# Turning blocks 1 to 3 of x by VectorE and DRAM instead of TensorE, in an adaLN linear-attention and MLP block

## The chip, the cores and the metric

The kernel runs on one core of one Trainium2 chip. The metric is the device time of one execution in microseconds (us). The kernel before took 1138.91 us (median of 3 runs, 1138.76 to 1139.21).

## The reference

One block of a transformer on 2048 tokens of width 576. The parts that matter here:

```python
h = _layernorm(x, axis=-1) * (1 + ca) + sa          # sa, ca, ga, ... from silu(c) @ w_mod
qkv = h @ wqkv                                       # 576 -> 3 x 576, 32 heads of 18
pq, pk = phi(q), phi(k)                              # where(t > 0, t + 1, exp(t)) + 1e-6
kv = einsum("bhsd,bhse->bhde", pk, v); z = pk summed over the tokens
x = x + ga * ((pq @ kv) / (pq . z + 1e-6)) @ wo
h = _layernorm(x, axis=-1) * (1 + cb) + sb
x = x + gb * silu(h @ w1) @ w2                       # 576 -> 4608 -> 576
```

## The kernel before, in words

The 2048 tokens are 16 tiles of 128, in four blocks (0 to 3) of four tiles. A tile has its tokens on the 128 partitions. A product with a weight needs the width on the partitions instead, so a normalised block has to be turned: from four tiles of 128 tokens x 576 into five chunks (k = 0 to 4) of 128 features x 512 tokens. The tail of 64 features is written twice, which makes a tile 640 wide (DX) and the fifth chunk full. Every f32 operand is then split into a rounded part ("hi") and a remainder ("lo"), and a product is three passes: hi x hi, hi x lo, lo x hi. `modulate` (L195) applies scale and shift per feature on ScalarE, `split_h` (L203) writes hi by a cast on ScalarE and lo by a subtraction on VectorE (through `sub_hi`, L121), both into the block's hT.

The first part (up to about 205 us) goes over the tiles t = 0 to 15 (L642). For each tile it makes the k product (`k_proj`, L552, from t = 2), the v product (`v_proj`, L561), the sum over tokens of the tile before (`kv_mm`, L582), and a q product (`q_proj`, L577) while any of the first eight are left. k, v and q all run through `x_passes` (L222 to L226), which is why they share the line L226 in the profile: k has 28 matmuls of 352 and 288 columns in turn, v (from t = 2) 14 of 512, q 28 of 288. Their PSUM tiles are called psK, of which there are two.

Block 0 is turned while the weights come in (`turn_tiles`, `turn_half`, L387 to L401). Block tb + 1 is loaded at t = 4 tb (`load_x`, tiles xt, four rooms), normalised at t = 4 tb + 1, and turned chunk by chunk at t = 4 tb + 2 and + 3 by `turn` (L633): four TensorE transposes of 128x128 into one PSUM tile psT (`transpose_chunk`, L212, matmuls of line L214), then `modulate_split`. So blocks 1 to 3 take 3 x 5 sets of four transposes.

The modulation vectors come from w_mod: for block 0's two, columns are summed on VectorE and reduced by TensorE (L355 to L385); the later ones are loaded in 576 KB pieces called raw, with one VectorE step each into tmod (L508 to L521). The loaded f32 weights lie in acc[0..14] (`load_w`, L289) until they are split; later acc[t] holds q of tile t. wo is loaded into acc[11..15] (`load_wo`, L604).

The order of the work is not left to the code's order. `arrange` (L107) takes a table ORDERS of instruction numbers per engine and ties each instruction to the one before it in the table. For PE the table keeps the code's order but for ten matmuls in the start, and PE stands under a manual schedule besides. Each engine carries out its list strictly in order, and so does SP, which issues nearly all DMAs: an entry that waits holds up all behind it. A DMA also waits until an earlier one that used the same of eight completion semaphores (DMAHW0 to 7 below) has landed. The second part (attention output and the first MLP group, to about 370 us) and the main loop over the MLP (L1542 and after) follow; the main loop's order is fixed by its PLAN.

Of the kernel before, what the change touches and what calls it, by code (L numbers as in the profile page):

```python
# [22 lines left out]
def kernel(ctx: ExitStack, tc, A_x, A_wqkv, A_wo, B_x, B_w1, B_w2, c, w_mod, out):  # L23
# [28 lines left out]
    def f32(ap):  # L52
# [4 lines left out]
            0-106 114 107-109 115 110-113 116-2586  # L57
        """,
        "DVE": """
            0 3 2 1 4 6-7 11 8 12-13 9-10 14-16 18 17 5 19-22 30 23-24 28-29 25-27 43 31 44 33-34 36 35 37-38 32 39  # L60
            41 40 42 45-47 50 48-49 62-63 51-53 57 84 64 55 58 65 59 86 66 85 87 60 56 80 67 88 81 83 68 82 69 71 70
            72 122 73-74 61 89 54 75 78 76 90 77 79 123 91 124 92-93 96-97 125 98 94 126-127 100 99 95 101 103-104
            107 105 108 106 109 111 102 132-133 135 110 134 136 138-139 137 140-144 112 145 148 113 146 149 147 114
            117 115 118 116 119-121 128-129 131 150-151 225 223 130 226 224 222 152-155 157-158 156 159 162 176 160
            177-178 161 179-181 163 165 228 227 166-167 164 169-170 168 171-173 193-197 199 198 200 202 201 203-205
            174 209 206-207 210 208 175 182 185 183 186 188 187 184 189-190 192 191 211-213 216 214 217 215 218 220
            219 221 229 232 230 233 231 234-237 240 238-239 241-243 246 244 247 245 248-249 252 250-251 253-256 258
            257 259 263 260-262 266 268 267 270 269 271 264-265 272-273 275-277 274 281 279 282 278 280 283-284 288
            285 289 286 295-296 290 306 303 302 291 307 292 314 293 315 294 297 323 304 298-299 324 308 331 287 300
            309 301 310-311 305 312 316 332 340 313 317-319 341 320-321 325 351 322 326-329 352 362 330 333-336 338  # L70
            363 337 339 344 370 345-347 342-343 349 348 353 371 380 354-359 350 360 381 361 398 364-369 399 416
            372-375 377 376 378 417 424 385 382 384 379 387-388 391-392 394 425 402 386 389 403 390 404-407 393 383
# [1520 lines left out]
```

## Time and profile before

| | us |
|---|---|
| median of 3 runs | 1138.91 |
| span of the profiled execution | 1136.9 |
| TensorE (PE) busy in it | 1126.8 |
| VectorE (DVE) busy | 971.0 |
| ScalarE (ACT) busy | 538.7 |
| GpSimd (POOL) busy | 649.3 |

The span runs from the first to the last instruction of the profiled execution; the runs' time also holds what lies outside it. In a timeline's row stand the start, the length, the engine, the line, what is written from what, the shapes and the number of instructions merged into the row; in brackets how long the engine was idle before, and what released it. PEld is TensorE's loading of weights. "SPq" is SP issuing a DMA. In a window's row stand the busy time of each engine and its number of instructions, the granted TensorE clock, the share of the DMA engines' time and the GB/s. Matmuls are pipelined, so the length of one is its latency; how fast they follow each other is read from the starts.

### The profile page before, as it was taken

The numbers are of one execution on the slowest core, as the hardware profiler recorded it, in microseconds if no ns is written. First come the engines' busy times: TensorE is split into PE (matmuls) and PEld (weight loads), VectorE is DVE, ScalarE is ACT, GpSimd is POOL, SyncE is SP. The second block draws the span as 40 slices with busy tenths as digits, with TensorE's granted clock in tenths as the row PEclk, the third lists the DMA queues.
The fourth block names the chain that finished last, engine by engine and source line by source line (L and its number), as shares of the span: only waits on it lengthen the run. The fifth ranks groups of instructions, "written<-read, shape, count | busy, mean of one in ns | idle before, by whom it ended". The sixth has DMA issues, their size and how long they took to land.

```text
span 1136.9 us, 19287 instructions
## 1 busy us (share of the span) xinstructions
PE 1126.8 (99%) x7033; PEld 1040.8 (92%) x7033; DVE 971.0 (85%) x1543; ACT 538.7 (47%) x1112; POOL 649.3 (57%) x743
## 2 busy tenths in 40 slices
PE   8999999999999999999999999999999999999998
PEld 7999999999998899999999999999989999999998
DVE  6866744686878899999999999999999999999996
ACT  5643442547556544445445444444444444444441
POOL 1100000374714777767775776677667767776786
PEclk9999999999999999999999999999999999999999
DMA  9621100223359877976978869779778697697684
GB/s 281 199 84 31 44 7 1 71 84 116 137 198 354 340 274 256 348 278 257 361 261 315 314 250 356 273 255 364 261 277 331 265 344 281 258 346 274 256 310 156
DMA packets 58813, 269.03 MB, mean 237 GB/s; under 512 B 5724, under 2 KB 21856, under 8 KB 35680
## 3 DMA queue, kind: packets, MB, share of 16 engines
q1 hardware_dynamic: 58708, 267.80, 64.4%
q8 instruction: 56, 0.92, 0.3%
q14 instruction: 37, 0.30, 0.1%
q10 hardware_dynamic: 12, 0.00, 0.0%
HBM read 250.12 MB, written 16.78 MB: 235 GB/s over the span
## 4 chain that ended last, share of the span: by engine, by line
PE 94%; DMA 3%; DVE 1%; ACT 1%; POOL 0%; SPq 0%; issue 0%; POOLq 0%
PE up L1324 34%; PE down L1397 32%; PE psK L226 12%; PE big L226 7%; PE small L886 2%; PE big L897 2%; PE kvp L589 1%; DMA hT<-in_w_mod_dram 1%; PE big L812 1%; DMA raw<-in_w_mod_dram 1%; DMA hT<-hd 1%; PE small L214 1%; DMA xt<-in_A_x_dram 1%; PE up L1427 1%; PE down L1427 1%; PE psT L214 1%
## 5 line engine op out<-in xcount | busy, mean ns | idle before, releaser
L1405 DVE TENSOR_TENSOR acc<-down,acc 128x576 f32<-128x576 f32 x330 | 246.2, 754 | 13.2 <-PE down L1397 3.2
L1324 PE MATMUL up<-hT,w 128*128 128x512 f32 x916 | 239.4, 390 | 0.5 <-DMA hT<-hd 0.5
L1324 PEld LDWEIGHTS up<-hT,w 128*128 128x128 f32 x916 | 164.5, 188 | 25.4 <-DMA hT<-hd 0.7
L1359 POOL TENSOR_TENSOR s<-f,f 128x256 f32<-128x256 f32 x66 | 52.3, 792 | 159.7 <-ACT f L1340 159.7
L1397 PE MATMUL down<-w,hb 128*128 128x288 f32 x792 | 120.6, 294 | 0.0
L1397 PE MATMUL down<-w,hc 128*128 128x288 f32 x792 | 120.6, 294 | 0.0
L1397 PEld LDWEIGHTS down<-w,hc 128*128 128x128 f32 x792 | 113.7, 188 | 5.4 <-PE up L1324 0.3
L1397 PEld LDWEIGHTS down<-w,hb 128*128 128x128 f32 x792 | 113.7, 188 | 5.3
L121 DVE TENSOR_TENSOR w<-v,w 128x288 fp32r<-128x288 f32 (+1 forms) x170 | 114.8, 684 | 2.8 <-ACT w L1058 2.8
L1405 DVE TENSOR_TENSOR U<-down,U 128x576 f32<-128x576 f32 x132 | 99.6, 754 | 17.1 <-PE down L1397 15.2
L226 PE MATMUL psK<-w,hT 128*128 128x352 f32 (+3 forms) x506 | 106.4, 336 | 1.1 <-POOL w L317 0.6
L1324 PE MATMUL up<-room,w 128*128 128x512 f32 x348 | 91.0, 390 | 0.0
L1378 POOL TENSOR_TENSOR hc<-s,hc 128x512 fp32r<-128x512 f32 x66 | 89.4, 1355 | 0.1
L184 POOL TENSOR_TENSOR rstd<-ve,neghalf 128x4 f32<-128x4 f32 (+3 forms) x10 | 9.5, 953 | 138.8 <-DVE ve L183 138.8
L226 PEld LDWEIGHTS psK<-w,hT 128*128 128x128 f32 x506 | 81.8, 188 | 7.5 <-POOL w L317 0.8
L1340 ACT ACTIVATE f<-f 128x512 f32<-128x512 f32 x102 | 64.5, 632 | 47.8 <-DVE f L1345 24.8
L1343 DVE TENSOR_TENSOR f<-up,p 128x512 f32<-128x512 f32 x102 | 69.7, 683 | 12.1 <-PE up L1324 11.2
L1066 ACT CAST w<-v 128x288 fp32r<-128x288 f32 x85 | 36.7, 434 | 76.4 <-PE down L1397 62.1
L1324 PEld LDWEIGHTS up<-room,w 128*128 128x128 f32 x348 | 62.5, 188 | 9.4
L1363 POOL TENSOR_TENSOR f<-f,s 128x256 f32<-128x256 f32 x66 | 51.2, 776 | 34.9 <-DVE hb L1378 24.5
L1397 PE MATMUL down<-w,he 128*128 128x288 f32 x396 | 63.0, 294 | 0.0
L1397 PE MATMUL down<-w,ha 128*128 128x288 f32 x396 | 63.0, 294 | 0.0
(310 smaller groups left out, 2529.7 us busy)
## 6 DMA issues: line engine op xcount, KB each, us to landing
hT<-hd SPq DMA_DIRECT2D x66, 1280.0 KB, 5.5
hT<-hd SPq DMA_DIRECT2D x45, 1024.0 KB, 5.5
room<-hd SPq DMA_DIRECT2D x35, 1280.0 KB, 5.7
room<-hd SPq DMA_DIRECT2D x20, 1024.0 KB, 5.1
v<-in_B_w_dram SPq DMA_DIRECT2D x17, 576.0 KB, 7.2
v<-in_B_w_dram SPq DMA_DIRECT2D x17, 512.0 KB, 7.1
hd<-S SPq DMA_DIRECT2D x6, 1024.0 KB, 3.8
xt<-in_A_x_dram SPq DMA_DIRECT2D x16, 288.0 KB, 5.2
```

Source lines behind the costliest of these rows:

```text
L121: return V.tensor_sub(lo, full, f32(hi))
L214: T.transpose(ps[:, i * P : (i + 1) * P], xt[i][:, cidx * P : (cidx + 1) * P], ident)
L226: T.matmul(ps, xpart(a), wpart(b), start=n == 0, stop=n == len(XW) - 1)
L1066: A.copy(self.w2[n][:, 0], src)
L1324: T.matmul(ps, left, right, start=first and m == 0, stop=m == len(seq) - 1, skip_group_check=True)
L1340: A.activation(self.f[i, k], self.f[i, k], AF.Silu)
L1343: V.tensor_add(f, self.bank[bank[1]], self.p1)
L1359: G.tensor_add(self.s[:, 0:1], half(i, 0, 1), half(i, 1, 1))
L1363: G.tensor_sub(half(i, 1, 0), half(i, 1, 0), self.s[:, 1:2])
L1378: eng.tensor_sub(t[:, :, 1, :], src, f32(t[:, :, 0, :]))
L1397: T.matmul(ps[:, p, :HALF], self.a[i, n][:, u, p * P : (p + 1) * P], self.w.w2[n][:, v], start=n in (1, 5, 7, 6) and j == 0, stop=j == 2, ...
L1405: V.tensor_add(dst, ps[:, :, :HALF], dst)
```

## The change

For blocks 1 to 3 TensorE's transposes are gone. Each normalised tile (128 x 640) is written by one VectorE instruction into a scratch tile with every square of 32x32 turned in itself (`turn_tile`). Four DMAs, one per group of 32 partitions, store it into a DRAM tile xd such that the squares land in their turned places: each writes 32 x 20 runs of 32 numbers (128 bytes). One DMA loads xd back into a chunked tile `turned` (128 features x 5 chunks x 512 tokens). `turn` then only modulates and splits a chunk out of `turned`, in place; the tile h32 and PSUM's psT are no longer used there. `turned` and three scratch tiles lie in the second half of acc, which is one tile now. They share room with the raw q weights and with wo, so the split of the q weights stands before the first `turn_tile` in the code, and wo is loaded at t = 12 instead of 10. With three scratch tiles for four tiles of a block, the fourth uses the first one's.

All manual schedules of PE up to the main loop's first two units are lifted, and ORDERS is new for all engines; it now has a full order for PE. The numbers of matmuls but for the transposes, and those of the 28 dummy matmuls of the start (`warm_up`), are the same.

```diff
     ORDERS = {
         "PE": """
-            0-106 114 107-109 115 110-113 116-2586
+            37 0-2 38 3 8 4-7 9-15 19-20 29-36 21 16 22 39 25 40 26 17 72 18 73 41 78 23 43 45 24 79 42 44 27 47 46 28
...
-    accb = [accp.tile([P, 4, D], F32, name=f"acc{b}") for b in range(NB)]
-    acc = [accb[t // 4][:, t % 4, :] for t in range(NT)]
+    acca = accp.tile([P, NT, D], F32, name="acc")
+    accb = [acca[:, 4 * b : 4 * b + 4] for b in range(NB)]
+    acc = [acca[:, t, :] for t in range(NT)]
...
-    with tc.manual_schedule(engines={mybir.EngineType.PE}):
+    with nullcontext():
...
+    free = acca[:, QB : NT, :].rearrange("p t d -> p (t d)")
+    turned = free[:, : (KC + 1) * 512].rearrange("p (c t) -> p c t", t=512)
+    squares = [free[:, (KC + 1) * 512 + n * DX :][:, :DX] for n in range(3)]
+    xd = [dram.tile([KC + 1, P, P], F32, name=f"xd{n}") for n in range(4)]
+
+    def turn_tile(i):
+
+        y, d = squares[i % 3], xd[i]
+        V.transpose(y, xts[i])
+        for a in range(4):
+            rows = slice(32 * a, 32 * a + 32)
+            nc.sync.dma_start(d[:, :, rows].rearrange("c (b j) t -> j (c b) t", j=32), y[rows].rearrange("j (b t) -> j b t", t=32))
+        nc.sync.dma_start(turned[:, :, i * P : i * P + P], d.rearrange("c p t -> p c t"))
+
     def turn(tb, k):
-        ps = psT()
-        transpose_chunk(xts, k, ps)
-        h32 = pa.tile([P, 512], F32, name="h32")
-        modulate_split(ps, k, hT[tb], cols["a"], h32)
+        modulate_split(turned[:, k], k, hT[tb], cols["a"], turned[:, k])
...
+            if t == 1:
+                for k in START:
+                    split_w(wqp_, k, acc[10 + k], V)
...
                     ln.normalise(j, xts[j], xts[j], A if j % 2 else V)
+                    turn_tile(j)
...
             if t == 1:
                 turn_half((4,))
-                for k in START:
-                    split_w(wqp_, k, acc[10 + k], V)
...
-            if t == 10:
+            if t == 12:
                 load_wo()
```

On PE, around the last chunk's turning of block 1 and the first product of tile 4. In before, psT_811 is the fifth set of block 1, kvp the sum over tokens of tile 2, psK_830 is q3 and psK_871 the k product of tile 4, whose hT_490 is block 1:

```order
L226 MATMUL psK_792<-w_106,hT_102 128x512 x2
L214 MATMUL psT_811<-ident_85,xt_394 128x128
L214 MATMUL psT_811<-ident_85,xt_396 128x128
L214 MATMUL psT_811<-ident_85,xt_398 128x128
L214 MATMUL psT_811<-ident_85,xt_400 128x128
L589 MATMUL kvp0_108<-pk0_150,vx0_152 128x256
```

```order
L589 MATMUL kvp2_110<-pk0_150,vx0_152 128x128
L226 MATMUL psK_830<-wq_107,hT_102 128x288 x28
L226 MATMUL psK_871<-w_103,hT_490 128x352
L226 MATMUL psK_871<-w_103,hT_490 128x288
```

In the changed kernel psK_820 is q3, psK_861 the k product of tile 4, and hT_520 block 1:

```order
L306 MATMUL psK_820<-wq_104,hT_99 128x288 x10
L670 MATMUL kvp1_106<-pk0_147,vx0_149 128x256
L306 MATMUL psK_820<-wq_104,hT_99 128x288 x5
L306 MATMUL psK_861<-w_100,hT_520 128x352
L306 MATMUL psK_861<-w_100,hT_520 128x288
L306 MATMUL psK_861<-v_101,hT_520 128x352
L306 MATMUL psK_820<-wq_104,hT_99 128x288 x2
L306 MATMUL psK_861<-v_101,hT_520 128x288
L306 MATMUL psK_861<-w_100,hT_520 128x352
L306 MATMUL psK_820<-wq_104,hT_99 128x288
```

The set is gone, and the k product of tile 4 begins with nine matmuls of q3 still to come, which stand among its own.

On VectorE, the changed kernel's steps from block 1's second transpose to its fourth, with what each waits for (`a<-psK` at L413 evicts the k product of tile 2, vx_149 at L200 its v product, tmod is a step of the modulation):

```order
L722 STREAM_TRANSPOSE acc<-xt 128x640 [waits DVE_49]
L722 STREAM_TRANSPOSE acc<-xt 128x640 [waits Activation_49]
L258 BN_STATS st<-xt 128x6 [waits DMAHW1_49]
L413 TENSOR_SCALAR a<-psK 128x576 [waits PE_49,Activation_49]
L200 TENSOR_TENSOR vx_149<-psK,vx_149 128x64
L258 BN_STATS st<-xt 128x6
L722 STREAM_TRANSPOSE acc<-xt 128x640 [waits DMAHW4_49,DMAHW5_49,DMAHW3_49,DMAHW2_49]
L200 TENSOR_TENSOR vx_149<-psK,vx_149 128x4x126 [waits Activation_49]
```

The same evictions in before:

```order
L333 TENSOR_SCALAR a<-psK 128x576 [waits PE_49,Activation_49]
L121 TENSOR_TENSOR vx_152<-psK,vx_152 128x64
L121 TENSOR_TENSOR hT<-h_661,hT 128x512 [waits Activation_49]
L519 SCALAR_TENSOR_TENSOR tmod<-raw,sc,tmod 128x2x576 [waits DMAHW5_49,DVE_49]
L121 TENSOR_TENSOR vx_152<-psK,vx_152 128x4x126 [waits Activation_49]
```

Between the two evictions there now stands a transpose that waits for four DMAs, the stores of the block's first tile; the subtraction for block 1's first chunk (hT) has left this place for a later one.

On ScalarE, in the start: in before the load of the Exp table follows block 0's first casts and comes ahead of tmod's columns.

```order
L205 CAST hT<-raw 128x256
L431 ACT_TABLE_LOAD
L431 ACTIVATE warm<-sc 128x1
L368 COPY tmod<-tmod 128x64
L368 COPY hT<-hT 128x2x64
```

In the changed kernel it stands right ahead of the first exponential (e), behind three casts of weights; the casts of the last two v weights, which GpSimd's subtractions need, come after it:

```order
L389 CAST w<-acc 128x576 x3
L271 ACTIVATE xt<-xt,nm,rstd 128x64
L406 ACT_TABLE_LOAD
L406 ACTIVATE e<-psK 128x576
L389 CAST v<-acc 128x576
L271 ACTIVATE xt<-xt,nm,rstd 128x64
L390 CAST w<-acc 64x576
```

The dummy exponential (warm) that loaded the table early has moved to a place behind block 1's modulation.

Two moves more, in words: on SP the last modulation columns of block 0 (hT, 128x2x320, L287 before) are issued ahead of the second k weight tile, not behind it; and on PE the last transposes of block 0's tiles 2 and 3 (L390 before) stand behind 11 matmuls of q0 and four of the first kv product, not ahead of both.

More of the change, by code (lines that the diff above doesn't have):

```diff
@@ L1 @@
-from contextlib import ExitStack
+from contextlib import ExitStack, nullcontext
 from itertools import count
@@ L58 @@
+            2509-2510 2505 2514 2511 2515-2518 2520 2519 2521-2526
         """,
         "DVE": """
[L60 to L63, printed above, removed]
@@ L537 @@
     NP0 = 2
+    QB = NT // 2
     def xsel(t):
@@ L687 @@
                 tm = mod_piece(t // 3)
-            if t == 10:
+            if t == 12:
                 load_wo()
-    with tc.manual_schedule(engines={mybir.EngineType.PE}):
+    with nullcontext():
         qs = iter(range(QB, NT))
@@ L1219, in attn_step @@
                 lns[tb].normalise(i, xn2[tb][i], acc[4 * tb + i], A if tb < 2 or i in (0, 1) else V)
-    with tc.manual_schedule(engines={mybir.EngineType.PE}):
+    with nullcontext():
         for s in range(NT + 2):
@@ L1547 @@
     units = [(g, p) for g in range(1, NG) for p in range(2)]
-    with tc.manual_schedule(engines={mybir.EngineType.PE}):
+    with nullcontext():
         fetch(5)
```

153 lines of the change are left out of this document (117 added, 36 removed).

## The prediction

> **What bounds the kernel now.** I read the page first (shares of the engines, chain of waits), then the windows of 20 us, then TensorE's timeline over the stage that changes.
>
> ```profile
> span 1136.9 us, 19287 instructions
> PE 1126.8 (99%) x7033; PEld 1040.8 (92%) x7033; DVE 971.0 (85%) x1543; ACT 538.7 (47%) x1112; POOL 649.3 (57%) x743
> PE 94%; DMA 3%; DVE 1%; ACT 1%; POOL 0%; SPq 0%; issue 0%; POOLq 0%
> 0.00:20.00 20.00, 18.21 (x123) 17.03 (x124) 12.41 (x34) 9.03 (x17) 4.07 (x13) 1.00 0.91 276
> 20.00:40.00 20.00, 17.32 (x127) 16.25 (x126) 16.95 (x39) 18.19 (x40) 4.34 (x3) 1.00 0.68 204
> 40.00:60.00 20.00, 19.52 (x136) 18.65 (x135) 18.24 (x36) 8.47 (x17) 1.05 (x1) 1.00 0.80 235
> 100.00:120.00 20.00, 20.00 (x137) 19.05 (x136) 15.68 (x22) 11.56 (x21) 0.00 (x0) 1.00 0.16 45
> ```
>
> TensorE (PE) works in 99% of the span, and the chain that ended last is PE for 94%. Its idle time lies in the start: 1.8, 2.7 and 0.5 us in the first three windows, 5.0 of the span's 10.1. From 60 us on a window holds 20.00 us of PE work. There an instruction taken off PE shortens the span by its full pace, if what PE multiplies next is ready; nothing else gains anything. So two questions decide: what is a transpose worth on PE, and will the turned block be there when PE asks for it?
>
> **What PE gives up.** The 60 transposes (15 sets of four) and two tiles' periods, one without and one with sets:
>
> ```profile
> L214 PE MATMUL psT<-ident,xt x60: 270/272/289, 50.4 to 164.1; 128*128 128x128 f32 x60
> 69.81 3.94 PE L226 MATMUL psK<-wq,hT 128*128 128x288 f32 x28
> 82.03 3.93 PE L226 MATMUL psK<-wq,hT 128*128 128x288 f32 x28
> 109.49 3.93 PE L226 MATMUL psK<-wq,hT 128*128 128x288 f32 x28
> 113.26 0.60 PE L214 MATMUL psT<-ident,xt 128*128 128x128 f32 x4
> 117.80 0.60 PE L214 MATMUL psT<-ident,xt 128*128 128x128 f32 x4
> 121.45 0.60 PE L214 MATMUL psT<-ident,xt 128*128 128x128 f32 x4
> 122.99 3.94 PE L226 MATMUL psK<-wq,hT 128*128 128x288 f32 x28
> ```
>
> Between two q projections (28 matmuls of 288) stand one k, one v and one kv product. Without a set that takes 82.03 - 69.81 = 12.22 us. With the sets at 113.26, 117.80 and 121.45 it takes 122.99 - 109.49 = 13.50. So a set costs 1.28 / 3 = 0.43 us, 0.11 a transpose (the 272 ns are its latency, not its pace). Fifteen sets: **-6.4 us**. They lie in a stretch in which PE never idles, bar one: the set at 50.37 stands ahead of the wait at 51.45 below, which would swallow its 0.43 if VectorE freed the bank no earlier. The new order of VectorE has no long step of tmod ahead of that eviction, so I count the set in full and the wait of 0.48 as gone too: **-0.5** (bounds 0.4 and -0.5).
>
> **The start.** PE's waits between 20 and 52 us, ScalarE's table load, and a cast at the end of ScalarE's queue there:
>
> ```profile
> 22.18 0.80 PE L407 MATMUL psK<-w,hT 128*128 128x288 f32 x4 [1.25 <-ACT hT L205]
> 23.15 0.79 PE L407 MATMUL psK<-w,hT 128*128 128x288 f32 x4 [0.18 <-DVE hT L121]
> 28.24 0.44 PE L390 MATMUL psT<-ident,xt 128*128 128x128 f32 x2 [0.68 <-ACT xt L191]
> 32.48 0.81 PE L226 MATMUL psK<-w,hT 128*128 128x256 f32 x4 [0.57 <-POOL w L317]
> 51.45 0.50 PE L226 MATMUL psK<-w,hT 128*128 128x512 f32 x1 [0.48 <-DVE acc L333]
> 13.92 1.28 ACT L431 ACT_TABLE_LOAD   x1
> 28.09 0.66 ACT L309 CAST v<-acc 128x576 fp32r<-128x576 f32 x1
> 220.00:370.00 150.00, 148.81 (x1052) 142.19 (x1051) 119.59 (x210) 88.52 (x159) 76.79 (x73) 1.00 0.49 175
> ```
>
> The waits of the first four rows sum to 2.7 us. Two moves act on them. The late modulation columns are now loaded ahead of the second k weight tile: 295 KB fewer before them, at the first window's 276 GB/s 1.1 us earlier, which the wait of 1.25 (for hT, made with these columns) could give back. Against it, the load of the Exp table, 1.28 us at 13.92 in a stretch where ScalarE had time, now stands right before the first exponential, among casts that follow each other without a gap up to 28.09 and that feed GpSimd, for which PE waits at 32.48. So -1.1 and +1.3: I take **0**, with -2.7 (every wait gone) and +1.3 (the table load in full) as ends. The order of the later stages is new as well, but from 220 to 370 us PE idles only 150.00 - 148.81 = 1.2 us, so I give it nothing.
>
> **The turned block's way.** A block's five chunks were made by PE, a step of ScalarE and so on, chunk by chunk. Now each tile takes a VectorE transpose, four stores of 80 KB in 640 runs of 128 bytes, a load of 320 KB, and then the same three steps per chunk. Blocks 2 and 3 are turned a whole tile period (12 us) before use, so their cost is hidden. Block 1 has no such room. The rows for it:
>
> ```profile
> 38.67 7.66 PE L226 MATMUL psK<-wq,hT 128*128 128x288 f32 x56
> 73.60 0.45 PE L226 MATMUL psK<-w,hT 128*128 128x352 f32 x2
> 37.65 0.81 SPq L260 DMA_DIRECT2D xt<-in_A_x_dram  x2
> 46.59 1.06 DVE L193 TENSOR_SCALAR xt<-xt,mv,rstd 128x576 f32<-128x576 f32 x2
> L1405 DVE TENSOR_TENSOR acc<-down,acc 128x576 f32<-128x576 f32 x330 | 246.2, 754 | 13.2 <-PE down L1397 3.2
> 13.47 0.55 DVE L360 TENSOR_SCALAR hT<-hT,sc 128x640 f32<-128x640 f32 x1
> 199.16 0.51 SPq L631 DMA_DIRECT2D a<-raw  x1
> pk<-raw SPq DMA_DIRECT2D x4, 72.0 KB, 2.1
> hd<-S SPq DMA_DIRECT2D x6, 1024.0 KB, 3.8
> acc<-in_A_x_dram SPq DMA_DIRECT2D x16, 288.0 KB, 2.7
> xt<-in_A_x_dram SPq DMA_DIRECT2D x16, 288.0 KB, 5.2
> L199 ACT ACTIVATE h<-psT,col_a x15: 772/785/798, 51.1 to 164.5; 128x512 f32<-128x512 f32 x15
> 51.92 0.62 ACT L205 CAST hT<-h 128x512 fp32r<-128x512 f32 x1
> ```
>
> *When PE needs it.* q0 starts at 38.67 and the first product of tile 4 (the first of block 1) at 73.60; with five sets and the wait gone that is 73.60 - 2.15 - 0.48 = 71.0. Nine of q3's 28 matmuls (0.135 each) now stand behind its start, which brings it to 69.8; its last chunk is due some 5 us later, about 74.7.
>
> *When it comes.* Tiles 2 and 3 were loaded at 37.65, once block 0's last transposes had freed their room. Those now stand behind 11 matmuls of q0 and four of kv, 2 us later: load at 39.7. Normalised tiles were there 10.0 us after the load (46.59 + 1.06), so 49.7. A transpose of 128x640 I price at 0.75 us, as the 754 ns of a 128x576 addition (bounds: 0.55, the 128x640 of one input at 13.47, and 1.5, two passes of the 754); four with the evictions that stand between them are through at about 55.5. SP issues a DMA of 32 partitions in 0.51; 16 stores and four others fill its queue from 50 to 60. A store lands after between 2.1 us (72 KB from 32 rows) and 3.8 (1 MB to DRAM): I take 3, nearer to the row with its shape, so 63. The load back takes 2.7 to 5.2: 3.5, so 66.5. ScalarE then spends 0.78 + 0.62 on a chunk, 7.0 for five, with 1.5 of evictions between them: last chunk at 75, due at 74.7. VectorE cannot be much earlier either: it is busy for 18.24 of the 20 us from 40 to 60 already, and gets 3 more. So the new wait lies between 0 and 3, more if a step is slower than priced; I take **+1.5**.
>
> The rule in the Trainium skill, VectorE: DVE Perf Modes, section The three transpose paths, speaks against the change, with the section Rules for kernel authors: VectorE turns only squares of 32, and for a whole 128x128 it advises TensorE. It gives 311 ns for 128x128 on VectorE in bf16; by it, an estimate, the 60 would take 18.7 us instead of 9.0, block 1 would come 3 us later and the time would be 1136.5. No row here shows a VectorE transpose.
>
> **The sum.** Span 1136.9 - 6.4 - 0.5 + 0 + 1.5 = 1131.5. The runs' median, 1138.9, stands 2.0 above the profiled span (the time outside it), so **1133.5**.
>
> **The rivals.**
>
> *The start gains too (0.15).* Interleaved orders fill PE's 2.7 us of early waits, and block 1 waits no more than 1.5. For it: the bytes moved behind the columns. Against: the table load. 1133.5 - 2.7 = 1130.8, or 1129.3 without any new wait.
>
> *Block 1 is late and eats the gain (0.18).* A new wait in place of the old work: 3 to 8 us, because SP's queue is strictly in order. A load back waits for its tile's four stores to land, and behind it stand the next tile's stores; each of the steps above slips by half a microsecond or two. For it: six estimated steps with no slack at their end. Against: the new PE order holds back q3 and kv products as fill at that place. Time: 1133.5 + 3 to 7 = 1136.5 to 1140.5, mostly within 0.2% of before.
>
> *Slow small stores: slower than before (0.12).* One mechanism at one place: the transpose of block 1's fourth tile writes into the room of the first, so it waits for that tile's stores to land, and VectorE's evictions stand behind it.
>
> ```profile
> q1 hardware_dynamic: 58708, 267.80, 64.4%
> ```
>
> A mean packet here takes 0.644 x 16 x 1136.9 / 58708 = 0.20 us of an engine, at 4.6 KB. If one of 128 bytes cost as much, a store's 640 on 16 engines would land after 8.0 us instead of 3. The fourth transpose would slip from 55.5 to about 60, its own stores by 5 more: block 1 some 9.5 us later, 1133.5 + 9.5 = 1143.0. Each microsecond of landing above 3 counts about twice, so the gain of 5.4 is gone at 5.7 us, and 0.2% is lost at 6.9. Against it: rows of 1 to 2.3 KB carried 276 GB/s at a share of 0.91 in the first window, and the page's mean packet of 4.6 KB makes 4.6 / 0.20 x 16 = 368 GB/s at full share: no steep fall. And 72 KB landed in 2.1. The Trainium skill, DMA: Bandwidth & Descriptors, section Specifications, is on its side: below 512 bytes an engine reads, modifies and writes back. By that rule the stores would be this rival's; no row of before has a store so small.
>
> **How the numbers follow.** The forecast has 0.55 and covers 1131 to 1136. A difference of 0.2%, 2.3 us, is about what a measurement of this kernel can tell from none. Faster than 1136.6: the forecast and the start's case, 0.70. Within 0.2%: late block 1, 0.18. Slower than 1141.2: slow stores, 0.12. The range runs from 1129.5 (waits of the start gone, a new wait near 0) to 1140.5 (block 1 late by 7 more); the slow stores are left out.
>
> **What would show it.** Right: no psT transposes of blocks 1 to 3 on PE; a period with q, k, v and kv of 12.2 us also at 110 us; PE idle between 60 and 80 us of 1 to 2 us, released by ScalarE or VectorE writing hT; transposes of about 0.75 us; stores landing in 2 to 4 us; the start's window of 20 to 40 us as full as before. Wrong: a PE wait above 5 us there; VectorE idle behind a transpose that a store released; a start more than 2 us longer or shorter; new waits after 220 us.

## The result, and the profile after

The changed kernel takes 1164.64 us (median of 4 runs, 1163.76 to 1165.8) against 1139.06 for the kernel before on the same chip. The ratio is 1.0221, interval 1.0204 to 1.0237: slower by 2.2%, 25.6 us, where I had forecast 5.4 us faster. In the figures below one execution of no_dram_trip, of 2244 us, is left out of the ratio but not of the median. First the page of the changed kernel: the span, the engines, the packets of the DMAs and the chain.

```profile
span 1163.7 us, 19292 instructions
PE 1133.7 (97%) x6973; PEld 1041.7 (90%) x6973; DVE 991.7 (85%) x1555; ACT 538.8 (46%) x1112; POOL 651.2 (56%) x743
DMA packets 98174, 276.90 MB, mean 238 GB/s; under 512 B 37404, under 2 KB 61216, under 8 KB 75040
PE 81%; DVE 7%; DMA 6%; ACT 2%; SPq 2%; issue 1%; POOL 0%; DVEq 0%; ACTq 0%; POOLq 0%
```

TensorE (PE) has 60 instructions less, as planned, and yet is busy for 6.9 us more; its idle time went from 10.1 to 30.0 us. So of 26.8 us of span 19.9 are new idleness; the rest is busy time, 6.9 us more where 6.4 were to go, some 13 us by which the same matmuls took longer. The chain shows who makes PE wait: VectorE's share went from 1% to 7%, the DMAs' from 3% to 6%, and the issuing on SP, which had nothing, has 2%. The windows, in the columns of those shown of before, say where:

```profile
20.00:40.00 20.00, 16.34 (x99) 15.29 (x98) 16.22 (x31) 15.11 (x29) 4.50 (x3) 0.83 0.54 170
60.00:80.00 20.00, 15.94 (x96) 14.71 (x96) 12.96 (x26) 6.59 (x14) 0.73 (x1) 0.91 0.76 181
100.00:120.00 20.00, 17.48 (x99) 15.89 (x98) 11.05 (x27) 9.19 (x17) 1.01 (x1) 0.91 0.64 153
140.00:160.00 20.00, 16.49 (x96) 14.26 (x95) 8.96 (x17) 8.55 (x17) 1.17 (x1) 1.00 0.35 87
220.00:370.00 150.00, 144.32 (x1013) 136.54 (x1012) 113.79 (x194) 84.94 (x151) 74.38 (x71) 0.99 0.38 136
360.00:380.00 20.00, 16.35 (x102) 14.17 (x100) 18.40 (x23) 14.46 (x28) 15.13 (x14) 1.00 0.81 297
380.00:400.00 20.00, 19.72 (x101) 17.12 (x101) 17.20 (x27) 7.60 (x15) 3.67 (x5) 0.91 0.68 249
```

Three of these windows in before:

```profile
60.00:80.00 20.00, 20.00 (x132) 18.95 (x132) 13.66 (x33) 9.75 (x19) 1.01 (x1) 1.00 0.25 86
140.00:160.00 20.00, 20.00 (x127) 18.57 (x127) 8.21 (x15) 8.79 (x17) 1.17 (x1) 1.00 0.00 1
360.00:380.00 20.00, 20.00 (x111) 17.64 (x110) 19.03 (x31) 10.57 (x24) 12.19 (x16) 1.00 0.92 338
```

Two places, not one. In the first part, 4.1, 2.5 and 3.5 us are lost in three windows of 20 us that had been full; behind it, between 220 and 370 us, PE idles 5.7 us instead of 1.2, and in the window from 360 to 380, which overlaps that one, 3.7. The clock column holds most of the rest: 0.83 and 0.91 in some of the windows that have waits in them or just before them, where it was 1.00 in before.

PE's waits up to 215 us, summed by what released them:

```profile
PE psK L306 <- DVE vx L200: 5.8, 3, 2.1
PE psK L306 <- DVE a L413: 2.7, 1, 2.7
PE psK L306 <- DVE mv L259: 2.4, 1, 2.4
PE psK L306 <- DVE col_b L608: 1.4, 1, 1.4
PE psK L306 <- ACT hT L285: 0.2, 1, 0.2
```

I had expected one wait, for the turned block (hT). PE never waits for that by more than 0.2 us. The 2.7 us (a) lie in the start, at 28.03. Behind 60 us PE waits for VectorE: for evictions of v products (vx), for a step of the statistics right behind such an eviction (mv, at 107.25), and for a column of the modulation (col_b, at 147.71, which stood behind 3.29 us of VectorE's waiting for a load of w_o). All these came late because VectorE, or the ScalarE step ahead of it, stood behind something else. The timelines show behind what. VectorE, SP and ScalarE, blocks 1 and 2; in brackets the idle time ahead of the row:

```profile
52.17 0.84 DVE L722 STREAM_TRANSPOSE acc<-xt 128x640 f32<-128x640 f32 x1
58.13 0.84 DVE L722 STREAM_TRANSPOSE acc<-xt 128x640 f32<-128x640 f32 x1 [0.35 <-DMA xd<-acc]
...
85.30 0.84 DVE L722 STREAM_TRANSPOSE acc<-xt 128x640 f32<-128x640 f32 x1
97.56 0.84 DVE L722 STREAM_TRANSPOSE acc<-xt 128x640 f32<-128x640 f32 x1 [3.54 <-DMA xd<-acc]
105.30 0.82 DVE L258 BATCH_NORM_STATS2 st<-xt 128x6 f32<-128x288 f32 x2 [5.35 <-DMA xt<-in_A_x_dram]
...
53.42 3.75 SPq L725 DMA_DIRECT2D xd<-acc  x6
57.22 0.53 SPq L340 DMA_DIRECT2D xt<-in_A_x_dram  x1
60.55 3.77 SPq L725 DMA_DIRECT2D xd<-acc  x4
64.41 0.45 SPq L340 DMA_DIRECT2D xt<-in_A_x_dram  x1
68.29 2.90 SPq L726 DMA_DIRECT2D acc<-xd  x3
...
75.56 0.81 ACT L279 ACTIVATE acc<-acc,col_a 128x512 f32<-128x512 f32 x1 [7.55 <-DMA acc<-xd]
147.78 2.93 ACT L279 ACTIVATE acc<-acc,col_a 128x512 f32<-128x512 f32 x4 [5.82 <-DMA acc<-xd]
```

Block 1's first transpose starts at 52.17, its first chunk is modulated (L279) at 75.56: the trip takes 23.4 us. Block 2's takes 113.36 - 85.30 = 28.1, block 3's, from 117.12, 30.7. ScalarE stands 7.55 us ahead of block 1's first chunk and 5.82 ahead of block 3's, with its casts behind. The loads of the next block's x (L340) lie scattered among the stores on SP, so VectorE's statistics (L258) wait for x, 5.35 us in one place, and the fourth transpose of block 2 waits 3.54 for the stores of the first. The rows for the transfers, from the view of the tile and from that of the DMAs:

```profile
L725 SPq DMA_DIRECT2D xd<-acc x48: 303/508/3185, 53.4 to 139.5; - x48
L726 SPq DMA_DIRECT2D acc<-xd x12: 359/388/778, 58.4 to 144.0; - x12
  ACT acc L279: 14.0, 3
  DVE acc L722: 4.5, 3
xd<-acc SPq DMA_DIRECT2D x48, 80.0 KB, 3.2
acc<-xd SPq DMA_DIRECT2D x12, 320.0 KB, 4.1
```

The last two rows hold the medians from issue to landing, of those DMAs whose landing the trace has (5 of the 48 stores and 3 of the 12 loads back): 3.2 us for a store and 4.1 for a load back, where I had 3 and 3.5. The longest store took 3185 ns to issue, the median 508. In that time SP issues nothing else; why that one was so slow, no view says.

### The profile page after: what moved, and what is told of

Its sections match the earlier page's. It is cut to its first block, busy times and chain, and to the rows that moved or that the text cites. A ratio compares the mean times of both kernels' runs of the same rounds, so it can differ in the third digit from the quotient of the medians.

```text
span 1163.7 us, 19292 instructions
## 1 busy us (share of the span) xinstructions
PE 1133.7 (97%) x6973; PEld 1041.7 (90%) x6973; DVE 991.7 (85%) x1555; ACT 538.8 (46%) x1112; POOL 651.2 (56%) x743
## 4 chain that ended last, share of the span: by engine, by line
PE 81%; DVE 7%; DMA 6%; ACT 2%; SPq 2%; issue 1%; POOL 0%; DVEq 0%; ACTq 0%; POOLq 0%
PE up L1417 32%; PE down L1490 31%; PE psK L306 7%; PE big L306 5%; DMA xd<-acc 2%; SPq L725 1%; PE small L979 1%; DMA xt<-in_A_x_dram 1%; PE big L990 1%; DMA w<-hd 1%; DMA hT<-in_w_mod_dram 1%; PE kvp L670 1%; DMA acc<-xd 1%; ACT acc L279 1%; PE big L905 1%
## 5 line engine op out<-in xcount | busy, mean ns | idle before, releaser
L306 PE MATMUL psK<-w,hT 128*128 128x512 f32 (+3 forms) x506 | 117.5, 346 | 12.4 <-DVE vx L200 3.8
L200 DVE TENSOR_TENSOR w<-v,w 128x288 fp32r<-128x288 f32 (+1 forms) x170 | 117.1, 697 | 0.9 <-ACT w L1151 0.9
L306 PEld LDWEIGHTS psK<-w,hT 128*128 128x128 f32 x506 | 84.6, 194 | 20.3 <-issue 6.9
L1436 DVE TENSOR_TENSOR f<-up,p 128x512 f32<-128x512 f32 x102 | 69.6, 682 | 13.5 <-PE up L1417 11.6
L306 PE MATMUL big<-w,qT 128*128 128x288 f32 x352 | 71.4, 307 | 0.2
L1490 PE MATMUL down<-w,hd 128*128 128x288 f32 x396 | 63.9, 294 | 0.0
```

The costliest lines, as they stand in the source:

```text
L200: return V.tensor_sub(lo, full, f32(hi))
L306: T.matmul(ps, xpart(a), wpart(b), start=n == 0, stop=n == len(XW) - 1)
L1436: V.tensor_add(f, self.bank[bank[1]], self.p1)
L1490: T.matmul(ps[:, p, :HALF], self.a[i, n][:, u, p * P : (p + 1) * P], self.w.w2[n][:, v], start=n in (1, 5, 7, 6) and j == 0, stop=j == 2, ...
```

## The experiments

The theory after this look: two separate losses, one in the new order of the engines behind the first part, one in the trip through DRAM. The rivals: the late load of the Exp table as the source of everything that follows; one loss only, whose waits drag on; the 128-byte pieces.

**The order behind the first part, both ways.** second_part_old_order is the changed kernel with its order behind the first part put back; before_second_part_new is the kernel before with the new order there and nothing else. The tables' first lines that differ:

```diff
-  "PE": ... 1149 1155 1188 1167-1168 1184 1169 1189 1170 1192 ...
+  "PE": ... 1149 1155 1167-2526
```
```diff
-  "PE": ... 115 110-113 116-2586
+  "PE": ... 115 110-113 116-1226 1248 1227-1228 1244 1229 1249 ...
```

> The changed kernel with one thing undone: behind the first part (from the last half of q on, about 200 us) the instructions of every engine stand in the order of the kernel before; the first part, with the turning through DRAM, is untouched. Theory A (the new orders themselves cost time, wherever they stand): the start of the main loop lay 25.4 us late against 9.5 us at tile 15's k product, so about 15 us were lost in a stretch where nothing is turned; with the old order there 1148 to 1153 us. Theory B (the way through DRAM is late, and what comes behind only carries it on, as waits and a lower clock): 1161 to 1166 us.

> The kernel before, TensorE transposes and all, but with the instructions behind the first part in the order of the changed kernel. Theory A: the 15 us come here too, 1150 to 1156 us. Theory B: no more than 2 us from 1139, 1137 to 1141 us.

Measured: 1151.14 us (1149.83 to 1156.55), ratio 1.0128 (1.0101 to 1.0154); and 1150.55, ratio 1.0107 (1.0091 to 1.0123). So the new order costs 13.5 us taken out of the changed kernel, and 11.7 put into the kernel before, where no tile goes through DRAM. PE's longest waits of before_second_part_new from 220 to 425 us, and its windows:

```profile
PE small L842 <- DVE hT L77: 2.8, 2, 1.9
PE big L768 <- DVE v L273: 1.7, 1, 1.7
```
```profile
220.00:370.00 150.00, 141.84 (x982) 132.97 (x981) 120.39 (x196) 84.21 (x148) 78.02 (x73) 0.99 0.42 154
360.00:370.00 10.00, 8.09 (x36) 6.68 (x35) 9.85 (x11) 3.00 (x6) 5.93 (x4) 0.83 0.58 217
```

In the kernel before with its own order PE's waits there are four, of 0.2 to 0.4 us. Now 7.0 us go between 220 and 370 (150.00 - 141.84 = 8.2, against 1.2), spread over a few steps of VectorE that come late, and at 360 to 370 the clock stands at 0.83, which is 1.7 us more. The rest of the 11.7 is not accounted for.

**TensorE's order alone.** second_part_pe_old has the old order of PE behind the first part, and leaves the other engines' there as the change has them (the Exp table is loaded early in it).

> best_orders, computing all of it, with VectorE, ScalarE, GpSimd and SP behind the first part in the new order and TensorE alone in the old one. If the 12.5 us of the second part come from TensorE's new order (it asks for products before their inputs): 1148 to 1152 us. If they come from the orders of the engines that feed it, they stay: 1159 to 1164 us.

Measured: 1176.45 us, ratio 1.0314 (1.0284 to 1.0345). Both expectations missed. The new lists belong together: with PE's alone put back, PE waits for GpSimd's steps (3.9 us for pn) as well. Which engine's list makes the loss can't be read from exchanging this one.

**The trip.** no_dram_trip leaves out the 48 stores and 12 loads and lets the steps read VectorE's squares as they are, so that a block is turned only within its squares. Each of a block's four tiles has a room of its own in it, so no transpose waits for the stores of an earlier tile:

```diff
         y, d = squares[i % 3], xd[i]
-        V.transpose(y, xts[i])
-        for a in range(4): ...  nc.sync.dma_start(d[...], y[rows]...)
-        nc.sync.dma_start(turned[:, :, i * P : i * P + P], d...)
+        V.transpose(turned[tb % 2][:, i * DX : i * DX + DX], xts[i])
```

> The changed kernel with its 48 stores and 12 loads of the turning left out: VectorE still transposes squares, into a place of their own, and the split reads these (so the blocks of x are only turned within their squares of 32, and the output is not the reference's). All other orders stay. Theory B (the DRAM trip is what is late): the waits for blocks 1 to 3 and the SP queue's go, 8 to 15 us less, 1149 to 1157 us. Theory A: the first part's waits are mostly those of the orders, 0 to 4 us less, 1160 to 1165 us.

Measured: 1147.49 us, ratio 1.0078 (1.0061 to 1.0095). So without the trip the kernel takes some 17.1 us less.

**The Exp table.** exp_table_early puts the dummy exponential back to where it loads the table before block 0's columns are ready (ScalarE's table, `10-11` to `10 3 11`).

> The changed kernel with the small Exp of the start (it loads the table of Exp) put back to where ScalarE had it before the change, behind its second split of block 0, so that the table is there before tile 0's Exp. If the load of 1.28 us at 25.2 us stands on the path at the start (theory A's smallest part): 1162 to 1164 us, 1 to 2 us less. If it is covered: 1164 to 1165.5 us.

Measured: 1163.14 us (1162.14 to 1164.79) against 1164.64 (1163.76 to 1165.8); ratio 1.0219 (1.0203 to 1.0234) against 1.0221. The load then lies at 15.19 instead of 25.24. The medians differ by 1.5 us, but the runs overlap, and the ratios don't tell the two apart. In the profiled executions the early table puts the k product of tile 3 1.4 us ahead of the changed kernel's, and the end of the first part 0.2 us behind it. And second_part_old_order, with the late table, came to tile 3 no later (58.3 us) than best_orders below with the early one (58.9). So a price of its own for the table load is not shown, and it starts nothing bigger.

**Do the parts add up?** best_orders is the changed kernel with the second part's old order and the table early; no_trip_best_orders is the same without the transfers.

> The changed kernel, computing all of it, with both undoings that were tried alone: the old order behind the first part, and the small Exp early. If the parts add up: 1164.6 - 13.5 - 1.4 = 1149.7, 1148 to 1151.5 us. If the Exp's gain is covered by block 1's wait, as the lag of exp_table_early at tile 4 suggests: 1150 to 1152 us.

> best_orders with the way through DRAM left out as in no_dram_trip (output not the reference's): what the change would be worth if the transport cost nothing. If the parts add up: 1147.5 - 12.5 - 1.4 = 1133.6, 1132 to 1136 us, some 5 us under the kernel before, as 15 sets of four transposes at 0.43 us would have it. If something else in the new first part eats the gain: 1137 to 1139 us.

Measured: 1148.99 us, ratio 1.009 (1.006 to 1.012), and 1133.6, ratio 0.9958 (0.9942 to 0.9973). They do, within 1 us of what was expected; but for the order and the table load together that means 15.7 us, of which the 1.5 of the table is not shown. The longest of the last one's TensorE waits up to 215 us, and a window:

```profile
PE psK L183 <- DVE w L272: 1.6, 1, 1.6
```
```profile
60.00:80.00 20.00, 20.00 (x129) 18.57 (x129) 18.96 (x38) 10.98 (x22) 1.36 (x1) 1.00 0.21 72
```

A full window at clock 1.00, and so are those at 100 and 140 us, with VectorE's transposes in them. By TensorE's first step of the second part (for qT of tile 0, at 222.66 in before) this kernel is 6.47 us ahead: the 6.4 for the sets of transposes. That it fits to the tenth is partly luck, since up to there PE is busy 7.4 us less and idle 0.9 us more. Such starts make a table of where each kernel stands against before; here those of the k product of a tile, of qT, and of the main loop's 113th unit:

| us behind the kernel before | k, t = 4 | t = 5 | t = 8 | t = 10 | qT | main loop |
|---|---|---|---|---|---|---|
| changed kernel | 4.9 | 8.1 | 7.2 | 13.1 | 12.5 | 27.3 |
| best_orders | 3.1 | 6.3 | 5.3 | 10.7 | 9.8 | 10.0 |
| no_trip_best_orders | -4.6 | -1.8 | -7.2 | -5.6 | -6.5 | -6.4 |
| before_second_part_new | -0.6 | -0.6 | -0.6 | -0.9 | -0.7 | 11.8 |

The difference of the two middle rows is the trip's price: 8.1 us by t = 5 (block 1), 12.5 by t = 8 (block 2), 16.3 from t = 10 on (block 3). Each block pays, block 1 about half.

**Is it the wait for the data?** trip_aside issues all 60 transfers, with the loads back into a place that no step reads (four of the five chunks, 256 KB instead of 320); the steps read the squares. As in no_dram_trip, a block's tiles have four rooms, so the fourth transpose's wait for the stores (4.5 us of VectorE in the changed kernel) is gone as well.

```diff
-        nc.sync.dma_start(turned[:, :, i * P : i * P + P], d.rearrange("c p t -> p c t"))
+        nc.sync.dma_start(aside[tb % 2][:, i * 512 : i * 512 + 512]..., d[0:KC].rearrange("c p t -> p c t"))
-        modulate_split(turned[:, k], k, hT[tb], cols["a"], turned[:, k])
+        modulate_split(y, k, hT[tb], cols["a"], y)
```

> As no_dram_trip (the split reads the squares that VectorE wrote, so blocks of x are only turned within their squares and the output is not the reference's), but the stores and loads of the turning are issued as in the changed kernel, at their places in SP's order; the loads take four of the five column chunks and land where nobody reads them. What is left out is only the waiting for what they bring. Theory W (the split waits for a trip that takes long): within 3 us of no_dram_trip's 1147.5, 1146 to 1151 us. Theory Q (the 60 transfers hold up SP's queue, and with it the loads of x and of w_mod, or the memory): most of the 17 us stay, 1158 to 1165 us.

Measured: 1159.44 us, ratio 1.0178 (1.0142 to 1.0213). Of the 17.1 us only some 5 go with the wait for the data and the transpose's wait; some 12 stay with the transfers alone (the runs spread over 1156.18 to 1162.61). VectorE's wait for x in this kernel from 44 to 160 us, and SP's timeline:

```profile
DVE st L135 <- DMA xt<-in_A_x_dram: 9.7, 6, 5.3
```
```profile
53.80 3.66 SPq L602 DMA_DIRECT2D xd<-acc  x6
...
60.74 4.32 SPq L602 DMA_DIRECT2D xd<-acc  x4
65.16 0.45 SPq L217 DMA_DIRECT2D xt<-in_A_x_dram  x1
```

Without a reader of the turned block, 9.7 us still go to waits for x (8.5 in the changed kernel, none in no_dram_trip). SP issues from 53.4 to 72.5 almost without a gap, four stores alone in 4.32 us, and the loads of x (L217) stand where their turn comes.

**Another queue, and x ahead.** Both start from best_orders. turn_on_gpsimd_queue issues the 60 transfers from GpSimd (`nc.sync.dma_start` to `nc.gpsimd.dma_start`, orders to suit). x_loads_first moves the next block's x loads ahead of most stores on SP:

```diff
 DMA raw<-in_w_mod_dram 128x1152 x3
 DMA xt<-in_A_x_dram 128x576
-DMA xd_386<-acc 32x20x32 x4
-DMA xd_388<-acc 32x20x32
-DMA xd_387<-acc 32x20x32
-DMA xt<-in_A_x_dram 128x576
+DMA xd_386<-acc 32x20x32
+DMA xt<-in_A_x_dram 128x576
+DMA xd_386<-acc 32x20x32 x3
+DMA xd_388<-acc 32x20x32
+DMA xt<-in_A_x_dram 128x576 x2
```

> best_orders, computing all of it, with the 60 transfers of the turning issued on GpSimd's queue and not on SP's: the loads of x, w_mod and w_o stand on SP alone again, in the same order. GpSimd has three operations in this stretch, the power of each block's variance, and the transfers of a block stand behind that block's. Theory Q (what SP's queue holds up, the next block's x above all, on whose statistics VectorE waits in order, is most of the loss): of the 15.4 us between best_orders and no_trip_best_orders about 12 go, 1136 to 1141 us. Rival (the traffic itself, or the trip's own time, or GpSimd's slower issue): 1144 to 1151 us.

> best_orders, computing all of it, with nothing moved but the eight loads of x for blocks 2 and 3 on SP, 5 to 12 places forward, ahead of stores of the turning (at about 0.5 us of SP for a store, 2 to 6 us). Theory Q in its narrow form (x's loads, through VectorE's statistics): 3 to 8 us less than best_orders, 1141 to 1146 us. If it is the loads of w_mod or the traffic: 1147 to 1150 us.

Measured: 1152.55 us (1150.47 to 1153.61), ratio 1.0107 (1.008 to 1.0134), and 1157.47 (1155.25 to 1159.28), ratio 1.0148 (1.0116 to 1.0181), against best_orders' 1149.0. VectorE's waits for x are gone in both, and neither is faster: x_loads_first is some 8 us slower than best_orders, and both lie above every range that I had given. ScalarE's wait for the turned block, of best_orders and of x_loads_first:

```profile
ACT acc L156 <- DMA acc<-xd: 13.7, 3, 7.8
```
```profile
ACT acc L156 <- DMA acc<-xd: 20.3, 3, 7.8
```

What x gains, the turned block loses: 13.7 us of waiting became 20.3. On GpSimd's queue it is 16.9. The trip is long whichever queue carries it: from block 1's first transpose to its first chunk's modulation it takes 24.2 us on GpSimd's queue (48.37 to 72.55) and 23.7 on SP's in best_orders (50.15 to 73.83). GpSimd issues each store more slowly:

```profile
L602 POOL DMA_DIRECT2D xd<-acc x48: 682/682/1149, 49.5 to 138.8; - x48
```

**Longer pieces.** long_runs lets VectorE write its squares so that a row's five belong together: 640 bytes a piece in place of 128.

```diff
-        V.transpose(y, xts[i])
+        V.transpose(y.rearrange("p (b c t) -> p c b t", c=KC + 1, t=32), xts[i].rearrange("p (c b t) -> p c b t", c=KC + 1, t=32))
-            nc.sync.dma_start(d[:, :, rows]..., y[rows].rearrange("j (b t) -> j b t", t=32))
+            nc.sync.dma_start(d[a].rearrange("(b j) w -> j b w", j=32), y[rows].rearrange("j (b w) -> j b w", b=4))
```

> best_orders, computing all of it, with the turned squares laid out so that the transfers move pieces of 640 bytes instead of 128 (stores) and 512 (loads): VectorE writes a tile's squares grouped by their row of partitions, a store of 32 rows has 128 pieces and not 640, and the split reads 16 runs of 32 columns. The number of transfers, their bytes and their places stay, save 13 instructions around tile 9 that move by one to three places because a tile's run now holds all five chunks. If the many short pieces make the trip late: landings of the stores under 2.5 us and 3 to 7 us less than best_orders, 1143 to 1147 us. If the trip is late by its fixed time and SP's queue: within 1.5 us of best_orders.

Measured: 1150.17 us (1146.36 to 1151.43), ratio 1.0091 (1.0058 to 1.0123): no different from best_orders. The packets and the transfers' rows of long_runs:

```profile
DMA packets 72063, 276.91 MB, mean 241 GB/s; under 512 B 6684, under 2 KB 35104, under 8 KB 48928
```
```profile
L601 SPq DMA_DIRECT2D xd<-acc x48: 303/440/812, 50.8 to 131.3; - x48
DMA to landing us min/median/max: 1.8/3.6/6.0
```

Packets below 512 bytes fell to 6684, from the changed kernel's 37404. The last row takes stores and loads back together; the stores alone land after a median of 3.0 us, against 3.2 (5 of the 48 in each trace). The issue shrank, the longest from 3071 ns in best_orders to 812, the median from 506 to 440. At t = 8 this kernel was 4.7 us ahead of best_orders, and lost it again in block 3, where VectorE stood 5.2 us for w_o's loads. long_runs_late puts some of w_o's loads, and the steps that wait for them, behind block 3's transfers (SP's, VectorE's and ScalarE's tables):

> long_runs, computing all of it, with 19 places of VectorE's order, 13 of ScalarE's and 7 of SP's changed behind 135 us (from block 3's turning on): what stood behind the loads of w_o or behind block 3's loads back and needs nothing of them is taken ahead. long_runs was 4.7 us ahead of best_orders at tile 8 and lost it again at block 3, where w_o's loads must wait until block 3's last split is through, since a run of 640 bytes holds all five chunks. If that loss is the layout's own and goes with the order: 1149.0 - 4.7 = 1144.3, 1142 to 1147 us, and the short pieces are then 4 to 5 us of the 15.4. If the waits only move again, as in past_transfers: 1148 to 1151 us.

Measured: 1147.0 us (1145.2 to 1147.89), ratio 1.007 (1.0054 to 1.0087), the upper edge of what was expected. Longer pieces and this order together are worth some 2 us (and the interval overlaps with that of best_orders), not the trip.

**Orders that wait later.** past_transfers takes every VectorE and ScalarE step that waits for a transfer, or for a step on the trip, behind the steps that were ready; past_transfers_sp does it on SP too; long_runs_past joins the first's rule for VectorE and ScalarE with long_runs. VectorE's list of past_transfers against best_orders, around block 1's fourth transpose:

```diff
 STREAM_TRANSPOSE acc<-xt 128x640 x2
-BN_STATS st<-xt 128x6
 TENSOR_SCALAR a<-psK 128x576
 TENSOR_TENSOR vx_149<-psK,vx_149 128x64
-BN_STATS st<-xt 128x6
-STREAM_TRANSPOSE acc<-xt 128x640
+BN_STATS st<-xt 128x6 x2
 TENSOR_TENSOR vx_149<-psK,vx_149 128x4x126
 TENSOR_TENSOR vx_149<-psK,vx_149 128x8
+STREAM_TRANSPOSE acc<-xt 128x640
```

> best_orders, computing all of it, with TensorE, GpSimd and SP in the very same order and the same transfers. On VectorE and ScalarE, behind 44 us, instructions that stood behind one that waits for a transfer of x or of the turning (statistics, squares, splits) and need nothing of it were taken ahead of it, nothing else: 60 places of VectorE's order and 32 of ScalarE's differ. ready_first moved 177 and 121 places, the start among them, and lost. Theory L (the queue behind the first instruction that waits is part of the price): by the same arithmetic with landings 0.5 to 1 us longer than shown, 5 to 9 us less than best_orders at tile 15, and some clock: 1139 to 1144 us. Rival (the trip's length before block 1 and the traffic are all of it): 1147 to 1150 us.

> As past_transfers, and SP too may take up to three transfers ahead of one whose source is not there yet (16 of its places differ). By the arithmetic within 1 us of past_transfers; if SP's order is what holds the trip up, 2 to 4 us less than past_transfers: 1136 to 1141 us.

> long_runs, computing all of it, with the rule of past_transfers (VectorE and ScalarE alone, from 44 us on; SP as in long_runs). past_transfers was 3.4 to 6.0 us ahead of best_orders from tile 4 to tile 10 and gave all but 1.3 back by the end of the first part. If both gains hold: 1139 to 1143 us, about the kernel before. If the waits move: 1145 to 1150 us.

Measured: 1149.18 us (ratio 1.0082, 1.0055 to 1.0109), 1151.61 (1.0095, 1.0064 to 1.0126) and 1145.9 (1.0067, 1.005 to 1.0085). PE's waits up to 215 us, of best_orders, and then of past_transfers:

```profile
PE psK L183 <- DVE vx L77: 7.3, 3, 2.9
PE psK L183 <- DVE mv L136: 2.4, 1, 2.4
```
```profile
PE psK L183 <- ACT hT L162: 4.5, 1, 4.5
PE psK L183 <- DVE vx L77: 3.9, 2, 2.9
PE psK L183 <- DVE acc L290: 3.2, 2, 2.9
```

The waits at the heads of the queues are mostly gone (ScalarE's 13.7 us for the loads back are 0.5, VectorE's 9.8 us for x are 2.2), and in their place PE waits for the block itself, 4.5 us for hT: now the wait that I had looked for, since the evictions no longer stand behind it. The time is the same.

A fourth rule, ready_first, drew up VectorE's, ScalarE's and SP's lists anew by when each step could start, with ready_first_no_trip as its partner without transfers:

> best_orders, computing all of it, with the same instructions and transfers, TensorE in the same order; on VectorE, ScalarE and SP the first part was drawn up again by hand-written rule: going through the order of best_orders with the durations and landings that its trace shows (stores 3.3 us, loads back 3.9, x 3.2, issues 0.4 to 0.53), an engine takes the first of its next ten (ScalarE eight, SP two) instructions whose inputs are there, so that no engine stands behind a transfer while it has other work. Theory L (the trip is too long for the lead that the orders give it, and what costs is the queue behind the first instruction that waits, on VectorE for x's loads, on ScalarE for the loads back): the three waits of block 1 to 3 go, most of the 15.4 us between best_orders and no_trip_best_orders goes, 1134 to 1141 us. Rival (the traffic, or the trip's own length, which no order hides): 1145 to 1150 us.

> no_trip_best_orders (no stores and loads of the turning, output not the reference's) drawn up again by the same rule. It shows what the rule gains where there is no trip to hide: by its own arithmetic up to 6 us, half of them in the start; TensorE waited 3.4 us in all in the first part of no_trip_best_orders, so not more than about 4: 1129.5 to 1133.6 us. If ready_first falls by much more than this one, the order's gain there is the trip's.

Measured: 1166.4 us (ratio 1.0238, 1.0218 to 1.0257) and 1149.76 (1.0095, 1.0073 to 1.0117). Both lie above every range that I had given. The rule itself costs 16 us with no transfer in the program, 8 of them by tile 2 (53.2 us against 45.1 in no_trip_best_orders), so it tells nothing of whether an order can hide the trip; the pair's difference is 16.6 us once more. The best complete kernel with the turning by VectorE remains long_runs_past, 7.1 us behind the kernel before. No version found here beats it.

## Why the prediction was wrong

The parts, each from a pair of runs: -4.5 us for what TensorE no longer does (no_trip_best_orders, 1133.6 against 1138.1 for the kernel before on that chip), +15.4 for the trip (best_orders over it), +13.5 for the order behind the first part. That makes 24.4; measured, 25.6. What is left, 1.2 us, lies within the spread of the runs, and so does the 1.5 of the Exp table.

- *"-6.4"* for the fifteen sets was right as a sum: 6.47 at the end of the first part, with the luck told above. Of it the main loop loses some again: the profiled spans differ by 5.1.
- *"-0.5"* for the wait at 51.45 failed: the same wait of PE is still there, and longer, since the eviction that ends it (at 52.94) now stands right behind VectorE's first transpose (52.17).

```profile
53.71 0.50 PE L306 MATMUL psK<-w,hT 128*128 128x512 f32 x1 [0.73 <-DVE acc L413]
```

- *"From 220 to 370 us PE idles only ... 1.2 us, so I give it nothing"* failed, by 13.5 us. That idle time was a property of the old lists. It tells how little there is to gain from a new order, and nothing of what a new order can lose. I took a bound on the gain for a bound on both sides, and gave a part of the change that moves instructions on every engine neither a term nor a rival.
- *"Blocks 2 and 3 are turned a whole tile period (12 us) before use, so their cost is hidden"* failed, by 8.2 us of the 16.3. From the last transpose's end to the first split it takes 16.6, 15.0 and 12.5 us for the three blocks, more than the period on which I relied. More than that, I asked only whether the block would be there when PE wants it. What PE felt were the other queues: the statistics behind x, x behind stores, evictions behind a transpose that waits.
- *"+1.5"* (0 to 3) for block 1 failed, by 6.6 us. Some sizes were nearly right: 0.84 us a transpose (0.75), landing 3.2 and 4.1 (3 and 3.5). The block's first chunk was modulated at 75.56, where I had the load back there at 66.5. The transposes were through at 58.97 (55.5), and SP's queue was mis-sized: I had it full from 50 to 60, with 20 DMAs, and it issued from 53.0 to 71.8, 26 DMAs with x loads, w_mod's and loads back among the stores, so the last loads back went out from 68.29 on (63). And I left out the steps behind a waiting one: ScalarE standing 7.55 us at the first split, with the casts for the evictions behind it.
- *The start, 0,* can't be told from right. TensorE came to tile 2 2.6 us later than in before and to tile 3 0.4 us later, and the 1.5 us between the medians with the table late and early are not clear of the spread (I had 1.3 as the upper end).
- *The rival "slow small stores"* had the sign, and a place that shows (VectorE stuck behind the fourth transpose, 4.5 us in three blocks). But in block 1, for which it had its price, that wait was 0.35 us, so that its 9.5 stands near the measured 8.1 is luck. Its cause was wrong: the stores landed after 3.2 us and not 8, and pieces five times as long changed little. The Trainium skill, DMA: Bandwidth & Descriptors, section Specifications, says that below 512 bytes an engine reads, modifies and writes back; here stores of 128-byte pieces landed after 3.2 us and of 640-byte pieces after 3.0, so the landing shows next to nothing of it. What the longer pieces took away is time of issue.
- *The rule for whole 128x128 blocks* (the Trainium skill, VectorE: DVE Perf Modes, sections The three transpose paths and Rules for kernel authors) gave the right advice by another price. By its figure for bf16 the 60 blocks were, as an estimate, 18.7 us of VectorE; here twelve transposes of 0.84 make 10.1, and with the transfers left out (so with the squares not in their turned places) the kernel is 4.5 us faster than before. In the first part, what makes the change slower is the way through DRAM.

Three of the four signs announced as wrong came: VectorE idle behind a transpose that a store released, new waits after 220 us, and a start 2.6 us longer by tile 2 (0.4 by tile 3). The fourth, a PE wait above 5 us between 60 and 80, did not: there were two of 2.0 and 2.1.

What stays open: whether some order hides the trip. Six new orders moved its waits from queue to queue; the best of them won 3 us, together with the longer pieces. An earlier load of x, with more room for tiles, was not tried. How much of the 15.4 us is the queues and how much the traffic itself is open too. And it is not settled which list makes the second part's loss, only that it lies in those lists and not in the turning.

## What to carry to other kernels

When a change brings a new operation and a new order, price and test them apart: put the new order into the old kernel, and the old order into the new one. A full engine's small idle time bounds what an order can win, never what it can lose. And a detour by DMA isn't priced by its landing alone: count its issues on the queue and every step that stands behind a waiting one, on each engine, since the wait shows up under another name than the tile that is late.

## What the hardware showed

- A kernel with new waits can lose more than their length. Over windows of 10 us, what the granted clock lacks of 1.00 times the window sums to 10.2 us in the changed kernel (6.8 up to 220 us, 3.4 from there to 440), and to nothing over the same stretch in before and in no_trip_best_orders. That is most of the 13 us by which the same matmuls took longer; some 3 stay unexplained. That waits bring the clock down is read from where the low windows lie, in or just behind those with waits. Not every wait does it: the changed kernel's window at 140 us idles 3.5 us at 1.00, and best_orders, with 16.3 us idle up to 220, lost 1.7.
- VectorE turns the squares of 128x640 f32 in 0.80 to 0.845 us, 1.3 ns a column, close to an addition of 576 (0.754).
- One DMA of this shape takes SP 0.51 us to issue (0.39 for the load back), GpSimd 0.68 (0.87).
